# Eight tokens to a partition, one 128-token block and a new order in a linear-attention and ELU kernel

## The chip, the cores and the metric

The kernel runs on one core of a Trainium2 chip. The metric is the device time of one execution in microseconds (us), and lower is better. Three executions of the kernel before took 209.01, 209.1 and 213.92 us; their median is 209.1 us. A profile is one execution taken by the hardware profiler. Its engines are PE (TensorE matmuls; PEld is its weight loading), DVE (VectorE), ACT (ScalarE), POOL (GpSimd) and SP (SyncE, used here for DMA issue only).

## The reference, cut to what matters

There are 4 batches of 8 heads, 768 tokens and a head size of 64. Decayed linear attention goes in blocks of 64 tokens, and its output, heads side by side, goes through a two-layer network with an ELU.

```python
intra = (q_b @ k_b.T) * D          # D[i,j] = lam**(i-j) for i >= j, else 0; 64 x 64
out_b = intra @ v_b + (q_b * lam**(pos+1)) @ state
state = lam**64 * state + (k_b * lam**(63-pos)).T @ v_b
...
x = out as [4*768, 512]
h = x @ w_in                       # 512 -> 2048
g = where(h > 0, h, exp(min(h, 0)) - 1)
y = g @ w_out                      # 2048 -> 512
```

The first block of a batch has a state of zero, so the first 128 tokens need no state: one causal 128-token block with the decay `lam**(i-j)` gives the same values as two 64-token blocks.

## The kernel before, in words

The work is cut into 24 chunks of 128 tokens. Chunk g is token chunk g // 4 of batch g % 4, so chunks 0 to 3 are the first 128 tokens of the four batches. Chunks are handled in pairs (0, 2, 4 ... 22).

Nothing is scheduled by a planner at build time. `PROGRAM` is one string of words, and each engine executes its share of the words in that order. A set `ON` names the words that go to the other of two engines. A word is a kind, a pair or chunk number, sometimes a part, and after @ the PSUM banks that it opens:

- `L` loads a chunk of q or k (or a pair of v) through POOL's DMA queue with a cast to fp16; the pieces in memory are 256 bytes long, one token of one head. `wi` and `wo` load slices of the two weight matrices on the same queue. `H` loads a chunk uncast through SP and `C` casts it. `D` is a transpose by DMA, issued by SP.
- `T` and `t`: transposes of q and k on PE, and the copies of them out of PSUM. `S`: scores. `s` (and `z` for the first 64 queries of the first chunks): score times mask on DVE. `P` and `Q`: the products with v and with the state; `F` is a tiny DVE read that orders the two. `p`: the copy of the attention output to fp16, which is the network's input.
- `kd`: k times its decay. `U`: the products of decayed k and v. `M`: the state times lam^64, always on POOL. `u`: the new state, on DVE. For a pair of chunks these run as a chain `U`, `u.0`, `M.1`, `u.1`, then `M.0` of the next pair of the same batches.
- `A2:5` is the first matrix product of pair 2, piece 5 of 8 (8 matmuls). `x`: exp on ACT. `r`: relu on DVE or ACT. `m`: the ELU's join on DVE, which frees the PSUM bank and one of three buffers for exp results. `B7:3` is the second product of chunk 7, piece 3 of 4 (4 matmuls); `Ba` and `Bb` are halves of a piece. `o` and `st`: copy out and store.
- `W`: matmuls on zeros, which fill PE at the start.

Two things set the order around the change. Every engine, and POOL's DMA queue too, works strictly in the order of the words: an `M` that waits on POOL holds back the loads behind it. And at most eight of POOL's loads are under way; the ninth waits for the first.

In the first chunks `scores` makes three 64 x 64 products a head (late queries on late keys, late on early, early on early) into two kinds of banks (psS, psZ), `masked` and `masked_first` multiply them with masks that hold only the decay by key, and `evacuate_p` multiplies the decay by query (`qs`) in on the way out.

Of the kernel before, what the change touches and what calls it, by code (L numbers as in the profile page):

```python
# [99 lines left out]
def kernel(  # L100
# [545 lines left out]
```

## Time and profile before

| | us |
|---|---|
| median of the runs | 209.1 |
| the profiled execution | 208.75 |
| its span, first to last instruction | 206.6 |
| PE busy | 199.4 (97%) |
| DVE busy | 150.8 (73%) |
| POOL busy | 102.4 (50%) |
| ACT busy | 98.7 (48%) |
| first network matmul starts | 16.88 |

The profiled execution spends 2.15 us outside its span. Busy time is the time in which an engine executes something; for POOL it includes the issuing of DMAs here. PE is close to full, so a look at where PE waits, and for whom, says more than the other engines' shares.

### The profile page before, as it was taken

The numbers are of one execution on the slowest core, as the hardware profiler recorded it, in microseconds if no ns is written. First come the engines' busy times: TensorE is split into PE (matmuls) and PEld (weight loads), VectorE is DVE, ScalarE is ACT, GpSimd is POOL, SyncE is SP. The second block draws the span as 40 slices with busy tenths as digits, with TensorE's granted clock in tenths as the row PEclk, the third lists the DMA queues.
The fourth block names the chain that finished last, engine by engine and source line by source line (L and its number), as shares of the span: only waits on it lengthen the run. The fifth ranks groups of instructions, "written<-read, shape, count | busy, mean of one in ns | idle before, by whom it ended". The sixth has DMA issues, their size and how long they took to land.

```text
span 206.6 us, 6317 instructions
## 1 busy us (share of the span) xinstructions
PE 199.4 (97%) x2724; PEld 134.2 (65%) x2724; DVE 150.8 (73%) x251; ACT 98.7 (48%) x186; POOL 102.4 (50%) x107
## 2 busy tenths in 40 slices
PE   7888999999999999999999999999999999999993
PEld 2457887457656887676765686775666787767442
DVE  0498999959976789786677899768886377638730
ACT  3463589204730785645362286455332287557301
POOL 7997989889972999929940770360000000000000
PEclk9999999999999999999999999999999999999999
DMA  5999999999999999999999699674020041010007
GB/s 108 148 172 190 193 181 180 177 176 135 143 131 151 128 102 175 148 252 96 152 127 177 87 130 168 117 183 151 3 105 3 0 154 52 0 38 3 0 0 267
DMA packets 104443, 25.31 MB, mean 123 GB/s; under 512 B 95072, under 2 KB 101472, under 8 KB 104416
## 3 DMA queue, kind: packets, MB, share of 16 engines
q0 software_dynamic: 79008, 13.37, 101.4%
q1 hardware_dynamic: 25264, 11.54, 29.5%
q8 instruction: 21, 0.34, 0.7%
q14 instruction: 6, 0.05, 0.1%
q10 hardware_dynamic: 144, 0.00, 0.0%
HBM read 27.27 MB, written 6.29 MB: 162 GB/s over the span
## 4 chain that ended last, share of the span: by engine, by line
PE 91%; DVE 3%; DMA 3%; issue 1%; POOL 1%; ACT 0%; DVEq 0%; POOLq 0%
PE psH L487 41%; PE psM L520 40%; DMA kn<-in_k_dram 3%; PE psU L454 2%; PE psO L395 2%; PE psS L350 2%; PE psO L412 2%; DVE xt L430 1%; PE psO L383 1%; DVE ppz L362 1%; PE psTk L308 1%; POOL kn L290 1%; PE psMrest L558 0%; DVE loglam_p L185 0%; PE psTq L308 0%
## 5 line engine op out<-in xcount | busy, mean ns | idle before, releaser
L487 PE MATMUL psH<-xt,wi 128*128 128x256 f16 x768 | 91.5, 273 | 0.4 <-DVE xt L430 0.4
L495 ACT ACTIVATE e<-psH 128x512 f32<-128x512 f32 x96 | 55.5, 598 | 75.4 <-PE psH L487 44.8
L520 PE MATMUL psM<-wo,g 128*128 128x512 f16 (+1 forms) x384 | 90.3, 377 | 0.0
L487 PEld LDWEIGHTS <-wi 128*128 128x128 f16 x768 | 74.2, 98 | 16.0 <-issue 0.4
L506 DVE SCALAR_TENSOR_TENSOR g<-e,psH 128x512 f16<-128x512 f32 x96 | 63.3, 683 | 10.5 <-ACT psH L501 9.2
L520 PEld LDWEIGHTS <-g 128*128 128x128 f16 x384 | 36.5, 98 | 34.5 <-DVE g L506 0.2
L462 POOL TENSOR_TENSOR stt<-state,upp 128x512 f32<-128x512 f16 x20 | 21.9, 1101 | 31.5 <-DVE state L474 31.5
L499 DVE TENSOR_SCALAR psH<-psH 128x512 f32<-128x512 f32 x41 | 28.3, 694 | 8.2 <-ACT e L495 7.8
L501 ACT ACTIVATE psH<-psH 128x512 f32<-128x512 f32 x55 | 32.3, 596 | 0.0
L290 POOL DMA_DIRECT2D kn<-in_k_dram x24 | 22.0, 925 | 2.4 <-DMA wi<-in_moe_w_in_dram 1.5
L430 DVE TENSOR_TENSOR xt<-psO,qs 128x512 f16<-128x512 f32 x24 | 15.6, 684 | 8.8 <-PE psO L412 7.7
L290 POOL DMA_DIRECT2D qn<-in_q_dram x22 | 19.9, 916 | 0.0
L529 ACT COPY osb<-psM 128x512 f32<-128x512 f32 (+1 forms) x16 | 9.2, 580 | 21.3 <-PE psM L520 21.3
L358 DVE TENSOR_TENSOR pp<-psS,mask 128x512 f16<-128x512 f32 x24 | 16.2, 682 | 2.7 <-PE psS L350 2.6
L474 DVE TENSOR_TENSOR state<-stt,psU 128x512 f16<-128x512 f32 x20 | 13.4, 681 | 2.4 <-PE psU L454 1.6
L442 POOL TENSOR_TENSOR kd<-kn,ks 128x1024 f16<-128x1024 f16 (+1 forms) x7 | 14.3, 2050 | 0.9 <-DMA kn<-in_k_dram 0.9
L290 POOL DMA_DIRECT2D vn<-in_v_dram x12 | 14.3, 1188 | 0.0
L547 PE MATMUL psW<-zeros 128*128 128x512 f16 (+1 forms) x36 | 10.0, 431 | 1.2 <-DVE zeros L540 1.2
L529 DVE COPY osb<-psM 128x512 f32<-128x512 f32 x8 | 5.5, 690 | 6.2 <-PE psM L520 6.2
L547 PEld LDWEIGHTS <-zeros 128*128 128x128 f16 x36 | 3.7, 112 | 5.8 <-issue 2.8
L442 DVE TENSOR_TENSOR kd<-kn,ks 128x1024 f16<-128x1024 f16 (+1 forms) x5 | 6.5, 1309 | 0.0
L293 POOL DMA_DIRECT2D wi<-in_moe_w_in_dram x8 | 6.2, 824 | 0.0
(56 smaller groups left out, 80.5 us busy)
## 6 DMA issues: line engine op xcount, KB each, us to landing
out_dram<-osb SPq DMA_DIRECT2D x23, 256.0 KB, 2.6
kn<-in_k_dram POOLq DMA_DIRECT2D x24, 128.0 KB, 6.1
vn<-in_v_dram POOLq DMA_DIRECT2D x12, 256.0 KB, 8.6
qn<-in_q_dram POOLq DMA_DIRECT2D x22, 128.0 KB, 5.9
wi<-in_moe_w_in_dram POOLq DMA_DIRECT2D x8, 256.0 KB, 9.4
wo<-in_moe_w_out_dram POOLq DMA_DIRECT2D x8, 256.0 KB, 6.3
raw_q<-in_q_dram SPq DMA_DIRECT2D x2, 256.0 KB, 4.6
qT<-qn SPq DMA_TRANSPOSE x18, 5.0
```

Source lines behind the costliest of these rows:

```text
L290: nc.gpsimd.dma_start(out=dst, in_=source(w, g0, n))
L358: nc.vector.tensor_tensor(out=p[:], in0=psS.pop(g)[:], in1=m[:], op=ALU.mult)
L430: nc.vector.tensor_tensor(out=xg[g0][:, :, a + s : a + 4 : 2, :].rearrange("p k i t -> p i k t"), in0=psO.pop((g, s))[:], in1=qs[:].unsque ...
L442: (nc.vector if f"kd{g}" in ON else nc.gpsimd).tensor_tensor(out=kds[g][r], in0=of("k", g)[r], in1=ks[r].unsqueeze(2).unsqueeze(3).broadca ...
L462: nc.gpsimd.tensor_tensor(out=t[:], in0=state[b, 2 * cb + s][:], in1=upp[:].unsqueeze(2).broadcast_to([128, H, 64]), op=ALU.mult,)
L487: nc.tensor.matmul(pH[:, f * n * 128 : (f + 1) * n * 128], lhsT=wi16[i][:, kk, w * 128 : (w + 1) * 128], rhs=xg[g0][:, kk].rearrange("p a ...
L495: nc.scalar.activation(es[g0, j][:], psH[g0, j][:], AF.Exp)
L499: nc.vector.tensor_scalar_max(psH[g0, j][:], psH[g0, j][:], 0.0)
L501: nc.scalar.activation(psH[g0, j][:], psH[g0, j][:], AF.Relu)
L506: nc.vector.scalar_tensor_tensor(out=g[:].rearrange("p f c t -> p (f c t)"), in0=es.pop((g0, j))[:], scalar=-1.0, in1=psH.pop((g0, j))[:], ...
L520: nc.tensor.matmul(psM[g][:, cols], lhsT=gts[g, f], rhs=wo16[i][:, w, cols], start=f == 0, stop=f == NFT - 1, skip_group_check=True,)
L529: (nc.vector.tensor_copy if on_dve else nc.scalar.copy)(o[:], src)
```

## The change

For chunks 0 to 3, q and k are loaded a second way: partition 16 h + o holds tokens 8 o to 8 o + 7 of head h, so that each piece in memory is 2 KB long. Chunks 0 and 1 (`H`) come uncast through SP, chunks 2 and 3 (`G`) as fp16 through POOL; both are then copied into tiles `oct` by `C`. The transposes work on pairs of such tiles, one for each of the eight token places, and the copies out of PSUM put the tokens back in order with a stride. The ordinary loads of k (`Lk0` to `Lk3`) stay, for `kd`, at later places; the old loads of q for chunks 0 to 3 (two raw ones on SP, `Lq2` and `Lq3`) go away.

The scores of the first chunks are one 128 x 128 product a head, in two halves of four heads (`Sz`, `S`), and the products with v are also in two halves (`Pz`, `P`). The mask of these chunks, 128 x 128 for each head, now holds the causal cut and the whole decay: eight exps on ACT (`dcz`, `dcs`) and two products on DVE (`mkz`, `mks`). So `p` is a plain copy there, on ACT for pair 0 and on DVE for pair 2. `llp` moves to ACT.

`PROGRAM` and `ON` are new throughout. 34 instead of 41 relus are on DVE, 7 instead of 5 `kd` (kd0, kd2 and kd4 among them, which POOL did before) and 9 instead of 8 `o`.

```diff
+EIGHTS = [('k', 0), ('k', 2), ('q', 0), ('q', 2)]
...
+    def decays(heads):
+        for h in heads:
+            nc.scalar.activation(mask1[:, h, :], dist[:], AF.Exp, scale=loglam[:, h : h + 1])
+    def mask_first(heads):
+        m = mask1[:, heads.start : heads.stop, :]
+        nc.vector.tensor_tensor(
+            out=m, in0=m, in1=cau1[:].unsqueeze(1).broadcast_to([128, len(heads), L]), op=ALU.mult
+        )
...
+    def eights(w, g):
+        c, b = divmod(g, B)
+        x = {"q": q, "k": k}[w][b, :, c * L : (c + 1) * L]
+        p = g - g % 2
+        if (w, p) not in oct:
+            oct[w, p] = buf(f"oct{w}{p}", [128, 8, 2, 64], FP16, f"oct{w}{p}")
+        return x.rearrange("h (o j) d -> h o (j d)", j=8), oct[w, p][:, :, g % 2]
...
+    def load_eights(w, g):
+        raw[w, g] = buf(f"stg{w}{g}", [128, 8, 64], FP16, f"stg_{w}{g}")
+        nc.gpsimd.dma_start(out=flat(raw[w, g][:]), in_=eights(w, g)[0])
...
+        if (w, g) in EIGHTS:
+            src = src.rearrange("p j x -> p x j")
+            dst = tr[w, g][:].rearrange("p h (o j) -> p (h o) j", j=8)[:, :, r.start : r.stop]
...
+    def scores_first(g, heads, store, banks):
+        for i in range(2):
+            store[g + i] = bank(banks[i], [128, H // 2, L], FP32, f"psS{g + i}_{heads.start}")
+        for n, h in enumerate(heads):
+            for i, d in enumerate(R):
+                nc.tensor.matmul(
+                    store[g + i][:, n, :], lhsT=tr["k", g][d, h, :], rhs=tr["q", g][d, h, :],
+                    start=True, stop=True, skip_group_check=True,
+                )
...
+    def first_chunk_products(g, x, banks):
+        psO[g, x] = bank(banks[0], [128, NHP // 2, 2, L], FP32, f"psO{g}_{x}")
+        for i in range(2):
+            for n in range(NHP // 2):
+                for c, rc in enumerate(R):
+                    nc.tensor.matmul(
+                        psO[g, x][rc, n, i, :], lhsT=vof(g + i)[:, x * NHP + 2 * n + c, :],
+                        rhs=(pp if x else ppz)[g + i][:, 2 * n + c, :], start=True, stop=True,
+                        skip_group_check=True,
+                    )
...
+        if g < B:
+            (nc.vector.tensor_copy if f"p{g}.{s}" in ON else nc.scalar.copy)(
+                xg[g0][:, 2 * s : 2 * s + 2, a : a + 4, :].rearrange("p k a t -> p k (a t)"),
+                psO.pop((g, s))[:].rearrange("p k i t -> p k (i t)"),
+            )
+            return
```

The two orders, as far as the prediction speaks of them (a line of dots marks what is left out):

```diff
-    "wz W0@0 W1 W2 W3 W4 W5 W6 W7 W8 W9 W10 W11 W12 W13 W14 W15 Lk0 lam Lk1 tab Lv0 Lk2 iota Hq0 "
-    "Lk3 ln row Lq2 Lq3 pos1 wi7 wi2 Lv2 wi1 wi6 Hq1 wi3 Cq0 pos0 pos5 dn1 pos2 pos3 cau1 idn "
-    "pos4 wi0 wi4 W16 W17 W18 Cq1 Tqa0@1 Tka0@2 tqa0 tka0 Tkb0 Tqb0 W19 W20 W21 W22 tqb0 llp tkb0 "
-    "S0@3,4,5,6 W23 W24 W25 qs dn W26 W27 W28 W29 ks kd0 msk1 W30 Tk2@7 tk2 W31 up W32 Tq2@1 tq2 "
-    "cau s1 msk z0 s0 z1 P0@2,4 p0.0 p0.1 S2@5,3,7,6 z3 A0:7@1 A0:2@2 s2 z2 s3 P2@4,6 p2.0 p2.1 "
-    "U0@5,7 W33 W34 W35 A0:1@3 x0:2 x0:7 r0:2 u0.0 r0:7 m0:7 m0:2 A2:7@0 x0:1 r0:1 wo0 Lq4 A2:2@4 "
-    "wi5 x2:2 x2:7 r2:7 r2:2 A0:6@6 A2:1@5 A2:6@1 m0:1 x0:6 r0:6 m2:7 m2:2 m0:6 x2:1 A0:0@2 "
-    "A2:0@3 x2:0 r2:1 m2:1 A2:4@0 r2:0 m2:0 x2:6 A2:3@4 A0:4@6 r2:6 x0:0 m2:6 r0:0 x2:4 Lk4 kd2 "
-    "Lk5 M0.1 wo6 x2:3 Ba2:0@5 Lq5 Ba3:0@3 m0:0 r2:3 u0.1 m2:3 A0:3@1 A0:5@2 Tk4@7 x0:4 r2:4 m2:4 "
...
+    "Hq1 wz W0@0 W1 W2 W3 W4 W5 W6 W7 W8 W9 W10 Hk0 wi2 Gq2 Gk3 iota pos0 row idn Gk2 Gq3 pos1 "
+    "pos2 dis Lv0 lam tab wi0 Lv2 wi1 wi5 Lq4 wi6 Lq5 wi3 Lk4 cau1 wi4 wi7 Lk5 ln dcz up Ck0 Lk0 "
+    "wo0 Lk1 wo1 wo2 wo3 Hq0 pos3 Cq0 Hk1 Ck1 W11 W12 W13 W14 W15 W16 W17 W18 Tka0@1 W19 Cq1 "
+    "Tqa0@2 Tkb0@3 dcs W20 tqa0 tka0 Cq2 Ck3 tkb0 cau pos4 mkz mks W21 Tqb0@4 tqb0 Ck2 Cq3 W22 "
+    "W23 W24 W25 W26 W27 Sz0@5,6 W28 Tka2@7 tka2 Tqa2@1 S0@2,3 W29 Tkb2@4 z0 W30 Tqb2@5 tqa2 tkb2 "
+    "z1 W31 W32 Pz0@7 s0 s1 P0@6 tqb2 Sz2@1,2 z2 S2@4,3 W33 W34 p0.0 p0.1 W35 A0:0@5 z3 Pz2@7 s3 "
+    "A0:2@6 s2 P2@0 p2.0 dn x0:2 p2.1 r0:2 A0:1@1 x0:1 m0:2 A2:2@2 r0:1 x0:0 r0:0 A2:0@3 x2:2 "
+    "r2:2 m2:2 m0:0 m0:1 A2:5@4 A0:6@7 x0:6 r0:6 Tq4@0 x2:0 r2:0 A0:5@6 x0:5 A2:6@2 A2:1@5 m2:0 "
+    "r0:5 ks x2:6 r2:6 m0:5 m0:6 m2:6 x2:1 r2:1 A0:3@1 msk A2:3@3 x0:3 A0:7@6 m2:1 x2:5 r2:5 r0:3 "
+    "Tk4@7 A2:4@2 x2:3 r2:3 m0:3 m2:5 m2:3 tq4 A2:7@5 tk4 A0:4@1 kd0 x2:4 r2:4 x0:4 r0:4 Ba0:0@4 "
+    "S4@0,3 s4 s5 m2:4 Ba1:0@7 Bb0:0 Bb1:0 U0@0,3 Ba0:1 Ba1:1 u0.0 Lv4 wo5 Ba2:0@2 wo7 Ba3:0@0 "
+    "Bb3:1 Bb0:1 kd4 wo6 M0.1 Lk6 u0.1 M4.0 Lk7 x0:7 llp qs x2:7 Bb2:0 r2:7 Ba3:1 r0:7 Bb1:1 m0:7 "
+    "m0:4 U4@3,6 Ba2:1 u4.0 Bb2:1 m2:7 Q4.1@1,3 F4 Bb2:2 P4 wo4 Bb0:3 Bb2:3 p4.0 p4.1 Bb0:2 Bb3:3 "
+    "Bb3:0 A4:0@5 Lk2 Bb3:2 A4:7@1 M4.1 Ba2:3 u4.1 x4:7 x4:0 r4:0 Ba3:2 A4:5@3 Ba3:3 Ba0:3 x4:5 "
+    "Ba0:2 Ba2:2 m4:0 Dk6.0 o3 r4:7 A4:1@6 Lq6 Lq7 x4:1 r4:5 m4:7 Lk3 kd2 M8.0 A4:3@5 r4:1 x4:3 "
+    "o0 r4:3 Ba1:2 A4:4@0 m4:5 A4:6@1 Lk8 o2 Dq6.0 U2@4,3 m4:3 m4:1 x4:6 Lv6 u2.0 r4:6 x4:4 r4:4 "
+    "kd6 U6@2,5 A4:2@6 x4:2 Dq6.1 B4:0@4 m4:6 r4:2 m4:4 Bb1:2 Lk9 B4:3 B4:2 Dk6.1 Lq8 Lq9 Dk8.0 "
+    "Lv8 Lk22 M2.1 u2.1 M6.0 kd8 B5:0@1 B5:3 m4:2 u6.0 Q6.1@0,3 F6 S6@6,2 Ba1:3 B5:1 s6 s7 P6 "
...
```

More of the change, by code (lines that the diff above doesn't have):

```diff
@@ L18 @@
 EARLY = 0
+EIGHTS = [('k', 0), ('k', 2), ('q', 0), ('q', 2)]
 BUFS = {'qn': 5, 'kn': 5, 'vn': 6, 'qT': 4, 'kT': 4, 'pp': 6, 'kd': 3, 'state': 6, 'stt': 3, 'xt2': 3, 'xt4': 2, 'e': 3, 'g': 40, 'osb512': 6}
 WARM = [512, 512, 512, 512, 512, 512, 512, 512, 512, 512, 512, 512, 512, 512, 512, 512, 512, 512, 512, 512, 512, 512, 512, 512, 512, 512, 512, 512, 512, 512, 256, 256, 256, 256, 256, 256]
-ON = {'Cq0', 'r14:6', 'r10:5', 'o17', 'r22:3', 'r0:0', 'r8:6', 'r20:6', 'r20:1', 'r0:1', 'r18:2', 'Cq1', 'o12', 'r12:4', 'o18', 'r6:6', 'r10:1', 'r4:7', 'r14:4', 'o19', 'r22:6', 'r14:5', 'kd20', 'lam', 'r2:1', 'kd18', 'r18:0', 'r2:5', 'r18:6', 'r16:7', 'r4:1', 'kd12', 'tqb0', 'r20:3', 'r18:7', 'r4:2', 'o4', 'r12:2', 'r22:0', 'o20', 'kd6', 'r2:0', 'r4:0', 'tqa0', 'o11', 'kd8', 'r14:1', 'r10:3', 'r8:2', 'r12:0', 'r6:2', 'r6:7', 'r18:5', 'r4:6', 'r0:3', 'r0:7', 'r0:4', 'r4:5', 'o13'}
+ON = {'r22:3', 'kd16', 'Cq3', 'r18:3', 'o18', 'r20:5', 'r22:4', 'kd0', 'o17', 'kd20', 'r16:5', 'r0:5', 'r8:6', 'r0:3', 'r8:4', 'r18:0', 'r10:7', 'r12:7', 'Ck2', 'r4:5', 'o19', 'r8:2', 'o13', 'r16:0', 'lam', 'r8:5', 'kd2', 'r20:3', 'p2.0', 'r0:1', 'Cq1', 'r16:2', 'r18:4', 'r10:5', 'o1', 'r22:6', 'r6:4', 'kd8', 'r12:1', 'r4:6', 'r0:0', 'o14', 'r2:2', 'r22:0', 'r18:2', 'tka0', 'kd14', 'r18:7', 'r10:1', 'r0:2', 'r14:6', 'o16', 'kd4', 'o3', 'r0:6', 'o0', 'p2.1'}
 PROGRAM = (
[56 rows of a table removed]
[57 rows of a table added]
 )
@@ L150 @@
     mask = const("mask", [128, H, LB])
-    cau1 = const("cau1", [128, LB])
-    dn1 = const("dn1", [128, H])
-    mask1 = const("mask1", [128, H, LB])
+    cau1 = const("cau1", [128, L])
+    dist = const("dist", [128, L])
+    mask1 = const("mask1", [128, H, L])
     qs = const("qs", [128, NHP, LB])
@@ L167 @@
     HEADS = {"": range(H), "a": range(H // 2), "b": range(H // 2, H)}
-    nat, raw, tr, psT, psS, pp, psO, xg = {}, {}, {}, {}, {}, {}, {}, {}
+    nat, raw, oct, tr, psT, psS, pp, psO, xg = {}, {}, {}, {}, {}, {}, {}, {}, {}
     kds, stt, psU, psH, es, gts, psM, osb = {}, {}, {}, {}, {}, {}, {}, {}
@@ L230 @@
         ),
-        "pos5": lambda _: nc.vector.tensor_scalar(
-            out=pos[:, 5:6], in0=pos[:, 0:1], scalar1=-1.0, scalar2=float(LB), op0=ALU.mult, op1=ALU.add
+        "dis": lambda _: nc.vector.tensor_scalar(
+            out=dist[:], in0=row[:], scalar1=pos[:, 0:1], scalar2=0.0, op0=ALU.subtract, op1=ALU.max
         ),
-        "dn1": lambda _: nc.scalar.activation(dn1[:], loglam[:], AF.Exp, scale=pos[:, 5:6]),
         "cau1": lambda _: nc.vector.tensor_scalar(
-            out=cau1[:], in0=row[:, :LB], scalar1=pos[:, 5:6], scalar2=0.0, op0=ALU.add, op1=ALU.is_ge
+            out=cau1[:], in0=row[:], scalar1=pos[:, 0:1], scalar2=None, op0=ALU.is_ge
         ),
-        "msk1": lambda _: nc.vector.tensor_tensor(
-            out=mask1[:],
-            in0=cau1[:].unsqueeze(1).broadcast_to([128, H, LB]),
-            in1=dn1[:].unsqueeze(2).broadcast_to([128, H, LB]),
-            op=ALU.mult,
-        ),
+        "dcz": lambda _: decays(HEADS["a"]),
+        "dcs": lambda _: decays(HEADS["b"]),
+        "mkz": lambda _: mask_first(HEADS["a"]),
+        "mks": lambda _: mask_first(HEADS["b"]),
         "ks": lambda _: nc.scalar.activation(ks[:], loglam[:], AF.Exp, scale=pos[:, 4:5]),
@@ L271, in vof, with flat @@
         return nat["v", g - g % 2][:, :, g % 2]
+    def eights(w, g):
[5 more added lines that the diff above has]
+        return x.rearrange("h (o j) d -> h o (j d)", j=8), oct[w, p][:, :, g % 2]
+    def flat(t):
+        return t.rearrange("p j d -> p (j d)")
     def load_raw(w, g):
-        raw[w, g] = buf(f"raw{w}{g}", [128, H, 64], FP32, f"raw_{w}{g}")
-        (nc.scalar if f"H{w}{g}" in ON else nc.sync).dma_start(
-            out=raw[w, g][:], in_=source(w, g, 1)
-        )
+        raw[w, g] = buf(f"raw{w}{g}", [128, 8, 64], FP32, f"raw_{w}{g}")
+        (nc.scalar if f"H{w}{g}" in ON else nc.sync).dma_start(out=flat(raw[w, g][:]), in_=eights(w, g)[0])
     def cast_raw(w, g):
-        t = nat_tile(w, g)[:, :, g % 2]
+        t = eights(w, g)[1]
         if f"C{w}{g}" in ON:
@@ L305, in transpose @@
         if banks[0]:
-            psT[w, g] = bank(banks[0], [128, H, 128], FP16, f"psT{w}{g}")
+            psT[w, part, g] = bank(banks[0], [128, H, 128], FP16, f"psT{w}{part}{g}")
         for h in HEADS[part]:
             nc.tensor.transpose(
-                psT[w, g][:, h, :], in_=of(w, g)[:, h, :, :], identity=ident16[:]
+                psT[w, part, g][:, h, :],
+                in_=oct[w, g][:, h, :, :] if (w, g) in EIGHTS else of(w, g)[:, h, :, :],
+                identity=ident16[:],
             )
@@ L316, in evacuate_t @@
         dst = tr[w, g][:, r.start : r.stop, :]
-        src = psT[w, g][:, r.start : r.stop, :]
+        src = psT[w, part, g][:, r.start : r.stop, :]
+        if (w, g) in EIGHTS:
+            src = src.rearrange("p j x -> p x j")
+            dst = tr[w, g][:].rearrange("p h (o j) -> p (h o) j", j=8)[:, :, r.start : r.stop]
         if f"t{w}{part}{g}" in ON:
@@ L330, in transpose_dma @@
         )
+    def scores_first(g, heads, store, banks):
[7 more added lines that the diff above has]
+                )
     def scores(g, banks):
+        if g < B:
+            scores_first(g, HEADS["b"], psS, banks)
+            return
         for i in range(2):
             psS[g + i] = bank(banks[i], [128, H, LB], FP32, f"psS{g + i}")
-        if g < B:
-            for i in range(2):
-                psZ[g + i] = bank(banks[2 + i], [128, H, LB], FP32, f"psZ{g + i}")
-            for h in range(H):
-                for kb, qb in ((1, 1), (0, 1), (0, 0)):
-                    for i, d in enumerate(R):
-                        nc.tensor.matmul(
-                            (psS if qb else psZ)[g + i][R[kb], h, :],
-                            lhsT=tr["k", g][d, h, R[kb]], rhs=tr["q", g][d, h, R[qb]],
-                            start=True, stop=True, skip_group_check=True,
-                        )
-            return
         for h in range(H):
@@ L355, in masked, with masked_part, out_bank @@
     def masked(g):
+        if g < B:
+            masked_part(g, HEADS["b"], psS, pp)
+            return
         p = pp[g] = buf("pp", [128, H, LB], FP16, f"pp{g}")
-        m = mask1 if g < B else mask
-        nc.vector.tensor_tensor(out=p[:], in0=psS.pop(g)[:], in1=m[:], op=ALU.mult)
-    def masked_first(g):
-        p = ppz[g] = buf("pp", [128, H, LB], FP16, f"ppz{g}")
-        nc.vector.tensor_tensor(out=p[R[0]], in0=psZ.pop(g)[R[0]], in1=mask[R[0]], op=ALU.mult)
-    def out_banks(g, banks):
-        for s in range(2):
-            psO[g, s] = bank(banks[s], [128, 2, NHP, LB], FP32, f"psO{g}_{s}")
+        nc.vector.tensor_tensor(out=p[:], in0=psS.pop(g)[:], in1=mask[:], op=ALU.mult)
+    def masked_part(g, heads, src, dst):
+        p = dst[g] = buf("pp", [128, H // 2, L], FP16, f"pp{g}_{heads.start}")
+        nc.vector.tensor_tensor(
+            out=p[:], in0=src.pop(g)[:], in1=mask1[:, heads.start : heads.stop, :], op=ALU.mult
+        )
+    def masked_first(g):
+        masked_part(g, HEADS["a"], psZ, ppz)
+    def out_bank(g, s, b):
+        psO[g, s] = bank(b, [128, 2, NHP, LB], FP32, f"psO{g}_{s}")
+    def first_chunk_products(g, x, banks):
[8 more added lines that the diff above has]
+                    )
     def products(g, banks):
@@ L377, in products @@
         if cb == 0:
-            out_banks(g, banks)
-            for s, rows, p in ((0, R[0], ppz), (1, slice(None), pp)):
-                for i in range(2):
-                    for hp in range(NHP):
-                        for c, rc in enumerate(R):
-                            nc.tensor.matmul(
-                                psO[g, s][rc, i, hp, :], lhsT=vof(g + i)[rows, 2 * hp + c, :],
-                                rhs=p[g + i][rows, 2 * hp + c, :], start=True, stop=True,
-                                skip_group_check=True,
-                            )
+            first_chunk_products(g, 1, banks)
             return
@@ L405, in state_products @@
         if part == 1:
-            out_banks(g, banks)
+            for s in range(2):
+                out_bank(g, s, banks[s])
             early[f"Q{g}.1"] = set(done)
@@ L429, in evacuate_p @@
         a = 2 * (g - g0)
+        if g < B:
+            (nc.vector.tensor_copy if f"p{g}.{s}" in ON else nc.scalar.copy)(
+                xg[g0][:, 2 * s : 2 * s + 2, a : a + 4, :].rearrange("p k a t -> p k (a t)"),
+                psO.pop((g, s))[:].rearrange("p k i t -> p k (i t)"),
+            )
+            return
         nc.vector.tensor_tensor(
@@ L573 @@
             simple[name](None)
-        elif kind in ("Hq", "Hk", "Hv"):
+        elif kind in ("Hq", "Hk"):
             load_raw(kind[1], *a)
-        elif kind in ("Cq", "Ck", "Cv"):
+        elif kind in ("Cq", "Ck"):
             cast_raw(kind[1], *a)
+        elif kind in ("Gq", "Gk"):
+            load_eights(kind[1], *a)
         elif kind in ("Lq", "Lk", "Lv"):
@@ L585 @@
             transpose_dma(kind[1], *a)
+        elif kind == "Sz":
+            scores_first(*a, HEADS["a"], psZ, banks)
         elif kind == "S":
             scores(*a, banks)
+        elif kind == "Pz":
+            first_chunk_products(*a, 0, banks)
         elif kind == "P":
```

2 lines of the change are left out of this document (1 added, 1 removed), and 86 rows, old and new, of the table PROGRAM.

## The prediction, made before the result was known

> **What bounds the kernel now.** I read the chain that ended last first, then the waits of PE, then the timeline of the first 60 us. By line the chain of the page's part 4 begins:
>
> ```profile
> PE 91%; DVE 3%; DMA 3%; issue 1%; POOL 1%; ACT 0%; DVEq 0%; POOLq 0%
> ```
>
> Nine tenths of the span are PE's own work. The longest pieces of that chain show where the rest is:
>
> ```profile
> 2.32 5.65 DMA kn<-in_k_dram
> ...
> 16.88 1.91 PE psH L487 x16
> 18.78 0.35 PE psO L383 x12
> 19.13 0.46 issue
> 19.59 0.62 PE psO L383 x20
> 20.21 0.38 PE psU L454 x32
> 20.59 0.43 PE psW L547 x3
> 21.02 9.61 PE psH L487 x88
> ```
>
> (start, length, what). Up to 16.88 the chain goes from the load of k through transposes, masks and DVE; at 16.88 the network starts, and from 21.02 PE is not idle again: the waits of PE, asked for from 40 to 65 us, are an empty list, and busy time by stretch gives PE 20.00 of 20 us from 42 to 62, 37.99 of 38 up to 100, 50.00 of 50 up to 150. So only two things can move the time: how much PE has done by about 21 us, and new waits of PE behind it. Matmuls cost the same in both kernels: 88 matmuls of A in 9.61 us are 0.873 us for a piece of 8, and the last 56 of B, 12.09 us, are 0.432 for a half.
>
> **The head.** The chunks' loads no longer decide it. SP issues its raw loads 0.51 us apart from 0.74, so the fourth starts at 2.3. Loads in 2 KB pieces are not in the trace; the stores of 256 KB are, with 2 KB pieces, and land in 2.6 us; the raw loads in 256-byte pieces landed in 4.1 and 5.0. That bounds the fourth load between 4.9 and 7.3; I take 6. Its cast on DVE (not shown for fp32 from SBUF; 0.42 for a 128x512 fp16 copy, 0.69 for any fp32 one) ends before 8. But PE can't begin its transposes before W18, and 19 W took from 1.19 to 7.53 us. From there I add up PE's own list up to A0:0: eight half transposes of 0.39 (3.1), eleven W of 512 at 0.22 (2.4), six of 256 at about 0.13 (0.8), four score blocks and two product blocks. The blocks are new in shape: 16 matmuls of 128 columns, against 8 transposes of 128 columns in 0.61 us, would be 1.2 one after another and 0.3 if they overlapped as fully as the 64 x 64 ones; two at a time, the nearest, 0.44, and 0.35 for a product block. Sum 8.8: **A0:0 at 16.3**, bounds 15.8 to 19. Beside it DVE (five casts, `tka0`, `mkz`, `mks` and four masks at a pitch of 0.61) is through with `s1` at 14.4 and ACT with `p0.1` at 15.9, so neither is late unless a load is. The mask's eight exps on ACT (0.34 each by the qs rows, 128x64) lie beside PE's W, and `p` of pair 0, an ACT copy of 0.6, takes the place of a DVE product of 0.69. Four loads are more than before (k of chunks 0 to 3 comes twice), and the small-piece loads of k move behind 20 us, where POOL's issue and PE's work hide them up to `kd0` and `kd2`, which are priced below.
>
> Behind A0:0 the kernel before lost time: its products of pair 2 waited for masks, and its third A started at 21.02. Now Pz2, A0:2, P2 and A0:1 follow with their masks done in time (`s2` ends at 18.1), and A2:2 follows `p2.1` at 19.65. By then three A and the products are done; before, that plus U0 (0.38) was done at 21.02 + 0.87. **Gain so far 1.9 us.**
>
> **The stage up to Q4.1.** Here the changed order does 16 A in a row and only then B, with U0 behind them; before, U0 came at 20.14, behind two A. DVE's list from `r0:2` (19.5) is 20 operations up to `m2:3`. The page's relu and ELU rows are 0.69 long, but follow each other at 0.61 (`g` x3 in 1.88): 12.1 us, to 31.6. Buffers of exp results and ACT leave no longer gap by my reading, list against list. PE, which needs those banks, reaches S4 at 32.6. Then `kd0`, on DVE now, 1.22 as at 60.77 (the cover that it had before, POOL, is gone); `s4` and `s5` to 34.5, and U0, which takes their banks, at 34.6; `m2:4`, `u0.0` to 35.8. Now the state's chain: M0.1 on POOL meets `kd4` on DVE. The trace has one such meeting:
>
> ```profile
> 45.93 3.02 POOL L462 TENSOR_TENSOR stt<-state,upp 128x512 f32<-128x512 f16 x2 [0.89 <-DVE state L474]
> 46.37 1.69 DVE L442 TENSOR_TENSOR kd<-kn,ks 128x1024 f16<-128x1024 f16 x1
> 54.81 0.45 PE L454 MATMUL psU<-vn,kd 64*64 64x64 f16 x32
> ```
>
> Two M in 3.02 us, the longest 2.01 against 1.03 else. So M0.1 ends at 37.85, `u0.1` at 38.55, M4.0 (behind Lk6) at 39.85, `u4.0` at 40.6: **Q4.1 at 40.7**. PE's own list from 16.3 gives 39.7 (16 A 14.0, 15 halves 6.5, products 0.7, two U 0.76, two transposes 1.0, S4 0.47), so PE waits 1.0 us here. Before, Q4.1 started at 41.69 with one half less done. The Trainium skill, page "SBUF — State Buffer", section "Who interferes with whom", says that a VectorE instruction with two SBUF inputs and a GpSimd one that reads SBUF exclude each other for the whole instruction; by that, M0.1 would only begin when `kd4` ends and everything behind it would be 0.6 us later still; the row above shows the slowing, and not whether one waits for the other's end.
>
> **The stage up to U6** decides. POOL's queue is in order: Lk6, Lk7, wo4, Lk2, Lq6, Lq7, Lk3, Lk8 and Lv6 stand behind M0.1, M4.0, M4.1 and M8.0. Before, `M0.1` was done at 25.1 and the vn of pair 6 was issued at 43.88, eleven us ahead of its U6 at 54.81 (third row above). Now POOL has nothing to do from about 30 (28 loads at 0.73 to 1.19 from 1.27) to 35.8. From M4.0's end at 39.85: Lk7 0.93, wo4 0.74, Lk2 0.93, M4.1 1.05, three loads 2.8, M8.0 1.05, Lk8 0.93: **Lv6 is issued at 48.25.** How long it takes is this row and its neighbours:
>
> ```profile
> vn<-in_v_dram POOLq DMA_DIRECT2D x1, 256.0 KB, 8.6
> ...
> DMA to landing us min/median/max: 6.6/8.4/13.3
> ```
>
> (the first from the DMA issues of 34 to 48 us, the second from the tile vn over the first 60 us; a single one from 60 to 80 us took 6.0.) By 8.4 it lands at 56.65. PE reaches U6 13.2 us after Q4.1 (7 A 6.1, 14 halves 6.05, U2, Q4.1, P4 together 1.1), at 53.9, and waits 2.7. `kd2` in front of it (k of chunk 3 issued at 45.4, landing 5.5, then 1.22) lets U2 go at about 53.5, as PE comes. So U6 is at 56.65, with one half (0.43) more done than before at 54.81: **1.4 us late**. A wait of 1 us at Q4.1 and 2.7 at U6 eats the 1.9.
>
> **The rest.** Behind U6 both lists hold the same A, B and attention work, and the loads of pairs 8 and 10 come 1 to 3 us before they are used by the same adding; I add nothing. Relus move 7 x 0.65 us from DVE to ACT, `kd` and `o` move some 4 us back; both engines have room (73% and 48%). The end is the same: 11 pieces of B after the last A against 14 before, each more than the evacuation of A needs.
>
> Sum: 208.75 + 1.4 = 210.2 for the profiled execution; the median of the runs before is 0.35 above it, so **210.5**.
>
> **Rivals.**
> - *The gain is kept.* POOL's loads have little beside them at 48 us, and Lv6 lands in 6.0: U6 at 54.25, 1.0 us ahead of before: 208.1. If the wait at Q4.1 went too, 207.1. For it: POOL's pause before 36 lets the DMA rings run empty. Against: 18 transposes by DMA and the small pieces of q and k fill the same engines (busy share of 9 tenths up to half the span).
> - *Slower: loads behind the state chain.* The same mechanism with 13.3, the longest landing of a v in this trace: U6 at 61.55, 6.3 us late: 215.4. It passes 2% (213.3) from a landing of 11.2. Lk9, Lq8, Lq9 and Lv8 stand in the same queue behind `kd6`, so it can strike again at U8. For it: POOL's order. Against: a median of 8.4.
> - *The new loads are not early.* Eight loads and wi2 start together; wi, in 1 KB pieces, took 6.1 to 11.1 to land. With 9 us the fourth raw load lands at 11.3, its transpose starts 3.6 to 4 us late, and all else with it: 1.4 + 3.6 gives 214. Against: only a few loads are under way at 2 us.
>
> **How the numbers follow.** Forecast (209.2 to 213.3) 0.48; gain kept (206.7 to 209.2) 0.27; loads behind the chain (213.3 to 216.5) 0.14; late raw loads (211 to 215) 0.08, half of it above 213.3; something faster than 204.9 that I don't see, 0.03: PE's list alone allows 16.3 + 23.4 = 39.7 at Q4.1, 2.4 us better than before with its extra half, not the 4.2 that 2% needs. 2% is about what a measurement of this kernel tells from no change. Range 207.4 to 214.3, which leaves out some 0.07 below and 0.10 above. Faster 0.03, same 0.79, slower 0.18.
>
> **What would show it.** In the profile after: first A at 16.3, and no gap of PE before the fourth A; a wait of PE for DVE around U0 to Q4.1; the vn of pair 6 issued near 48 and a wait of PE on it of 1 to 4 us near 55; PE full from there on. A first A at 18 or later, gaps of PE above 2 us before 41, or any idle PE behind 65 us would make the forecast wrong.

## The result and the profile after

The changed kernel is slower: a median of 216.78 us in four runs (216.02 to 217.43) against 210.45 in four runs of the kernel before. The ratio is 1.032, with a 95% interval of 1.022 to 1.043; it leaves out one disturbed run of the kernel before (213.92), which is why it is a little above the ratio of the two medians. The profiled execution took 216.02 us, its span 214.0, which is 7.4 us more than the span before.

The chain that ended last, by engine, from the page of the kernel after:

```profile
PE 61%; DMA 12%; DVE 10%; POOL 10%; issue 3%; ACT 1%; SPq 1%; DVEq 0%; POOLq 0%; ACTq 0%
```

It was nine tenths PE before. Now DMA, DVE and POOL carry a third of it. For the beginning I asked for the chain up to 62 us (start, length, what):

```profile
2.91 11.13 DMA raw_k<-in_k_dram
14.06 0.44 DVE octk L305
14.54 0.61 PE psTka L333 x4
...
23.68 0.87 PE psH L533 x8
```

The fourth raw load is issued at 2.91 and holds everything for 11.13 us. The network's first matmul, at 16.88 before, is at 23.51 (the chain shows its last stretch, from 23.68). PE's waits, over the first 24 us, name one new wait (line, releaser, us, times, longest):

```profile
PE psTka L333 <- DVE octk L305: 7.3, 1, 7.3
```

The longest waits of the head before were 1.2 us for the zeros, which is still there, and 0.8. The four casts of the raw loads, from the timeline of DVE and of ACT (start, length, engine, line, operation, then in brackets the idle time before it and what ended it):

```profile
6.42 0.60 ACT L303 CAST octq<-raw_q 128x512 f16<-128x512 f32 x1
...
8.60 0.43 DVE L305 CAST octk<-raw_k 128x512 f16<-128x512 f32 x1 [3.50 <-DMA raw_k<-in_k_dram]
...
11.71 0.43 DVE L305 CAST octq<-raw_q 128x512 f16<-128x512 f32 x1 [2.62 <-DMA raw_q<-in_q_dram]
...
14.06 0.43 DVE L305 CAST octk<-raw_k 128x512 f16<-128x512 f32 x1 [1.92 <-DMA raw_k<-in_k_dram]
```

The three on DVE each wait for their load, so their starts are the landings: 3.1 and 2.35 us apart, though SP issued the loads 0.6 to 0.9 us apart. (The first load, cast on ACT, was there by 6.42.) They do not land side by side but one after another.

Busy time by stretch shows a second effect. The columns are the stretch, then for PE, PEld, DVE, ACT and POOL the busy us and (instructions), then the granted clock, the DMA share and GB/s:

```profile
10.00:12.00 2.00, 0.00 (x0) 0.00 (x0) 0.29 (x1) 0.00 (x0) 0.76 (x1) 0.93 1.59 220
12.00:14.00 2.00, 0.00 (x0) 0.00 (x0) 0.14 (x1) 0.00 (x0) 0.74 (x1) 0.50 1.68 179
14.00:16.00 2.00, 1.46 (x11) 1.18 (x12) 1.24 (x3) 0.00 (x0) 1.43 (x2) 0.50 1.89 176
16.00:18.00 2.00, 2.00 (x13) 1.16 (x11) 1.94 (x6) 1.33 (x3) 1.84 (x3) 0.50 1.62 156
18.00:20.00 2.00, 2.00 (x16) 0.79 (x15) 0.15 (x1) 1.37 (x3) 0.89 (x1) 0.86 1.72 169
```

PE went idle at 7.3. About 4.5 us later the granted clock fell to a half, and it stayed there for 4 us after PE began its transposes. The Trainium skill, page "TensorE: Matmul & The Clock Gate", section "Part 1: The HAM clock gate (the "warmup" mystery)", says that the clock halves after an idle window of some 3.4 us and returns after as much sustained work; the rows above, 4.5 and 4 us, lie about a microsecond above that.

Where the time went, by stages (us; Q4.1 and U6 are those of the forecast, and the second column adds up the prediction's own steps):

| | predicted | measured |
|---|---|---|
| first A starts | 16.3 | 23.51 |
| first A to Q4.1 | 24.4 | 24.42 (to 47.93) |
| Q4.1 to U6 | 15.95 | 13.82 (to 61.75) |
| U6 to the end of the execution | 153.5 | 154.27 |
| sum | 210.15 | 216.02 |

So the head is 7.2 us later than forecast, and the stage up to U6 gives 2.1 of that back. The rest is 0.8.

### The profile page after: what moved, and what is told of

It is laid out like the page before. It is cut to its first block, busy times and chain, and to the rows that moved or that the text cites. A ratio compares the mean times of both kernels' runs of the same rounds, so it can differ in the third digit from the quotient of the medians.

```text
span 214.0 us, 6149 instructions
## 1 busy us (share of the span) xinstructions
PE 201.2 (94%) x2628; PEld 134.7 (63%) x2628; DVE 149.4 (70%) x248; ACT 105.6 (49%) x207; POOL 99.3 (46%) x107
## 4 chain that ended last, share of the span: by engine, by line
PE 61%; DMA 12%; DVE 10%; POOL 10%; issue 3%; ACT 1%; SPq 1%; DVEq 0%; POOLq 0%; ACTq 0%
PE psM L566 28%; PE psH L533 23%; DMA vn<-in_v_dram 5%; DMA raw_k<-in_k_dram 5%; DVE g L552 5%; POOL kn L315 2%; POOL stt L508 2%; DVE psH L545 2%; PE psW L593 2%; POOL qn L315 2%; POOL kd L488 2%; DMA kn<-in_k_dram 2%; PE psO L452 1%; PE psU L500 1%; POOL vn L315 1%
## 5 line engine op out<-in xcount | busy, mean ns | idle before, releaser
L508 POOL TENSOR_TENSOR stt<-state,upp 128x512 f32<-128x512 f16 x20 | 22.9, 1149 | 35.9 <-DVE state L520 27.1
L547 ACT ACTIVATE psH<-psH 128x512 f32<-128x512 f32 x62 | 36.5, 597 | 0.0
L545 DVE TENSOR_SCALAR psH<-psH 128x512 f32<-128x512 f32 x34 | 23.2, 694 | 9.1 <-ACT e L541 8.8
L315 POOL DMA_DIRECT2D qn<-in_q_dram x20 | 18.0, 908 | 0.6 <-DMA stg_k<-in_k_dram 0.6
L476 DVE TENSOR_TENSOR xt<-psO,qs 128x512 f16<-128x512 f32 x20 | 13.0, 685 | 5.8 <-PE psO L452 5.8
L391 DVE TENSOR_TENSOR pp<-psS,mask 128x512 f16<-128x512 f32 x20 | 13.1, 683 | 1.1 <-PE psS L381 1.0
L593 PE MATMUL psW<-zeros 128*128 128x512 f16 (+1 forms) x36 | 11.7, 460 | 1.2 <-DVE zeros L586 1.2
L488 POOL TENSOR_TENSOR kd<-kn,ks 128x1024 f16<-128x1024 f16 (+1 forms) x5 | 9.7, 1934 | 2.5 <-DMA kn<-in_k_dram 2.5
L488 DVE TENSOR_TENSOR kd<-kn,ks 128x1024 f16<-128x1024 f16 (+1 forms) x7 | 9.9, 1419 | 0.0
L333 PE MATMUL psTka<-ident,octk 128*128 128x128 f16 x8 | 1.0, 262 | 7.3 <-DVE octk L305 7.3
```

The source lines that it names most:

```text
L315: nc.gpsimd.dma_start(out=dst, in_=source(w, g0, n))
L391: nc.vector.tensor_tensor(out=p[:], in0=psS.pop(g)[:], in1=mask[:], op=ALU.mult)
L488: (nc.vector if f"kd{g}" in ON else nc.gpsimd).tensor_tensor(out=kds[g][r], in0=of("k", g)[r], in1=ks[r].unsqueeze(2).unsqueeze(3).broadca ...
L508: nc.gpsimd.tensor_tensor(out=t[:], in0=state[b, 2 * cb + s][:], in1=upp[:].unsqueeze(2).broadcast_to([128, H, 64]), op=ALU.mult,)
L545: nc.vector.tensor_scalar_max(psH[g0, j][:], psH[g0, j][:], 0.0)
L547: nc.scalar.activation(psH[g0, j][:], psH[g0, j][:], AF.Relu)
```

## The experiments

My theory: SP's queue passes the four raw loads one behind another, and beside POOL's first loads it gets only a part of the DMA engines, so that the fourth is late. Rivals: the shape of the pieces, the amount of POOL's bytes ahead of them, SP's queue alone, and the clock. Unless a median is given, a run below is one execution; executions of the kernel before lay between 208.66 and 214.22 us, so the readings rest on times inside the traces more than on the totals.

**POOL's loads held back.** A copy on POOL that waits for the fourth raw load stands ahead of all its loads; the raw loads are the first four on SP in any case.

```diff
-Hk0 wi2 Gq2 Gk3 iota pos0 ... Hq0 pos3 Cq0 Hk1 Ck1
+Hk0 Hq0 Hk1 iota hold wi2 Gq2 Gk3 pos0 ... pos3 Cq0 Ck1
+    def hold(_):
+        nc.gpsimd.tensor_copy(t[:], raw["k", 1][:, 0, :1])
```

> All loads of POOL's queue are held back until the fourth raw load has landed. Theory (the raw loads share the DMA engines with the loads that POOL starts at the same time, 1.6 MB by 8 us): with nothing beside them the four land one behind the other by 5 to 7 us, so the first transpose starts at about 7.5 instead of 14.5; the loads of chunks 2 and 3 and of the weights then come later, and the first network matmul may still not be early. Rival 1 (loads in 2 KB pieces on SP's queue are slow by themselves, some 2.7 us each): the fourth lands at 11 to 14 as before. Rival 2 (SP's queue passes only one load at a time): four steps of over 2 us, 10 us or later.

Measured: 219.29 us, first transpose at 11.22, first A at 26.59. The raw loads' casts, from the timelines of ACT and DVE:

```profile
5.63 0.62 ACT L303 CAST octq<-raw_q 128x512 f16<-128x512 f32 x1 [0.62 <-DMA raw_q<-in_q_dram]
...
7.36 0.43 DVE L305 CAST octk<-raw_k 128x512 f16<-128x512 f32 x1 [4.98 <-DMA raw_k<-in_k_dram]
...
9.07 0.43 DVE L305 CAST octq<-raw_q 128x512 f16<-128x512 f32 x1 [1.22 <-DMA raw_q<-in_q_dram]
10.74 0.43 DVE L305 CAST octk<-raw_k 128x512 f16<-128x512 f32 x1 [1.24 <-DMA raw_k<-in_k_dram]
```

All four start when their load lands, 1.7 us apart: 256 KB in 1.7 us is some 155 GB/s, with nothing else of size under way. So both explanations hold a part. Even alone the fourth lands at 10.7, not at the 5 to 7 that I expected; the sharing adds 3.3 us to that. The bytes by queue say the same. From the DMA view of 4 to 8 us (queue, packets, MB, share of 16 engines), first of this run, then of the kernel after, where q1 is SP's queue and q0 POOL's:

```profile
q1 hardware_dynamic: 333, 0.65, 53.1%
```

```profile
q0 software_dynamic: 683, 0.32, 74.2%
q1 hardware_dynamic: 232, 0.44, 37.4%
```

SP's queue moved 0.65 MB in 4 us alone, and 0.44 MB with POOL's queue beside it. Alone it kept the 16 DMA engines only 53% busy, so there it is not full engines that space the loads; what in the queue does is not shown. The time is worse than that of the kernel after because everything on POOL was held back: behind the first transposes PE waits another 4.79 us for the copies of the next chunks.

**Piece size.** The same loads in pieces of one token of one head (256 bytes), with the copies out of PSUM in plain order.

```diff
-return x.rearrange("h (o j) d -> h o (j d)", j=8), oct[w, p][:, :, g % 2]
+return source(w, g, 1), oct[w, p][:, :, g % 2]
```

> The same loads on the same queues in the same order, but in 256-byte pieces, one token of one head a partition and head (the transposes then give heads instead of token places, and the copies out of PSUM need no new order). Theory (the bytes under way decide): no earlier, first transpose at 14 to 18 us. Rival (large pieces on SP's queue are what is slow): first transpose near 8, as in the kernel before, and the first network matmul near 16 to 18.

Measured: 216.0 us, first transpose at 14.18, first A at 23.04. The piece size neither makes the loads late nor would cure them.

**Clock.** 32 more matmuls on zeros ahead of the first transpose.

```diff
+WARM += [512] * 32
-W18 Tka0@1
+W18 W36 W37 ... W67 Tka0@1
```

> 32 more matmuls on zeros between the last of the old ones and the first transpose (7 us), so that PE does not idle while it waits for the raw loads. Theory (the late load is the loss, and PE's half clock after the idle 7.3 us comes on top): the granted clock stays at 1.0 and the time from the first transpose to the first network matmul shrinks from 9.0 to 7 to 8 us, so 1 to 2 us of the 7.4 are the clock's. Rival (DVE and ACT set that stretch): 9.0 as it was, time unchanged at 216.

Measured: 215.55 us. The granted clock was 1.00 throughout. The last raw load landed 1.1 us later in this run (first transpose at 15.64), but first transpose to first A took 7.04 us instead of 8.97. The half clock costs 1.9 us of the head here; it follows from the idle PE and is not the cause.

**k on ACT's queue.** The two raw loads of k are issued by ACT, those of q by SP.

```diff
-Hk0 wi2 ... Hq0 pos3 Cq0 Hk1 Ck1
+Hk0 Hq0 Hk1 wi2 ... pos3 Cq0 Ck1
+ON has Hk0 and Hk1 (ACT issues them)
```

> The two raw loads of k go through ACT's DMA queue, and all four are issued at the start. Theory (shared engines): both queues get a share beside POOL's, so the fourth lands some 2 to 3 us earlier, near 11, and the time falls by as much, to 213 to 214. Rival 2 (one load at a time on SP's queue): two and two in parallel, the fourth lands near 7 to 8 us and the time falls to about 210.

Measured: 215.87 us, first A at 23.51 as in the kernel after; neither explanation had expected that. k of chunk 0 was cast at 5.27 and the first transpose came at 12.71 instead of 14.54, but the second load of q landed only at 11.89, and what was won was lost again. Part of that is a side effect of the edit: the small load of the decays is on ACT's queue too, now behind k. ACT read it at 3.48 in the kernel after, and here:

```profile
12.46 0.21 ACT L185 ACTIVATE loglam<-lam_b 128x8 f32<-128x8 f32 x1 [7.87 <-DMA lam_b<-in_lam_dram]
```

ACT then cast q of chunk 1 at 13.98 instead of 6.42, PE waited another 0.9 us for it, and the granted clock was 0.50 from 14 to 18 us. So this run does not tell what a third queue alone is worth.

**Only POOL's order.** The raw loads stay on SP; POOL's first loads are put in the order in which they are needed, the weights last.

```diff
-wi2 Gq2 Gk3 iota pos0 row idn Gk2 Gq3 ... Lv0 ... wi0 Lv2 wi1
+Gk2 Gq2 iota pos0 row idn Lv0 Gk3 Gq3 wi0 wi2 Lv2 ... wi1
```

> The four raw loads stay on SP; of POOL's first loads only the order is new: Gk2, Gq2, the tables, Lv0, Gk3, Gq3, wi0, wi2, Lv2, instead of wi2, Gq2, Gk3, the tables, Gk2, Gq3, Lv0, wi0, Lv2. Theory (the raw loads share the DMA engines with whatever else is under way, so fewer bytes beside them bring them in earlier): wi2 reads 512 KB and a G 256 KB; about 1 to 1.5 us less beside the raw loads, first transpose at 13 to 13.5 instead of 14.54, first A at 22 or so, time 214.5 to 215.5. Rival (SP's queue by itself passes them this slowly when any other queue has work): first transpose at 14.5, time 216.

Measured: 217.2 us, first transpose at 15.29, first A at 24.66. My theory failed here in its form "fewer bytes beside them": with other loads first on POOL's queue, the raw loads came no earlier, and even a little later than the rival had it. SP's casts on DVE were 2.9 and 2.7 us apart, as if the two queues took turns. The Trainium skill, page "DMA: Bandwidth & Descriptors", section "Queues, rings and completion order", says that each DMA engine goes round-robin between the queues that have work, a packet at a time. The bytes by queue fit that: from 4 to 8 us SP's queue moved 0.44 MB here, as in the kernel after, and 0.65 MB alone. The turns themselves are not in the trace.

**Two of the four on POOL.** As the run above, with k of chunks 0 and 1 loaded by POOL (first in its queue, in the same 2 KB pieces), so that SP carries only q.

```diff
-Hq1 wz ... Hk0 Gk2 Gq2 iota ... Hq0 pos3 Cq0 Hk1 Ck1
+Hq1 Hq0 wz ... Gk0 Gk1 Gk2 Gq2 iota ... pos3 Cq0 Ck1
```

> k of chunks 0 and 1 goes through POOL (as Gk0, Gk1, first in its queue, 2 KB pieces), so that SP carries only q; everything else is as in the order run. Theory (what was late is the fourth raw load, behind 768 KB on one queue and beside POOL's first loads): k0 and k1 land at 7 to 8, q0 at about 7.5, first transpose at 8 to 9, first A at 17 to 18, time 210 to 211: all 6 us or nearly all come back. Rival (the same 1 MB must be read for the pair, and the engines give it 150 to 200 GB/s whatever the queue): first transpose 11 or later, time 213 or above.

Measured: 210.12 us. From the timelines of DVE and PE:

```profile
7.92 0.29 DVE L305 COPY octk<-stg_k 128x512 f16<-128x512 f16 x1 [1.87 <-DMA stg_k<-in_k_dram]
...
9.04 0.43 DVE L305 CAST octq<-raw_q 128x512 f16<-128x512 f32 x1 [0.77 <-DMA raw_q<-in_q_dram]
9.38 0.29 DVE L305 COPY octk<-stg_k 128x512 f16<-128x512 f16 x1
...
9.72 0.40 PE L333 MATMUL psTka<-ident,octk 128*128 128x128 f16 x4 [2.33 <-DVE octk L305]
...
12.83 0.38 DVE L305 COPY octk<-stg_k 128x512 f16<-128x512 f16 x1 [1.78 <-DMA stg_k<-in_k_dram]
...
18.20 1.04 PE L533 MATMUL psH<-xt,wi 128*128 128x256 f16 x8
```

The second load of q is now the last of its queue and lands at 9.0; first transpose at 9.72, first A at 18.20, and the clock stayed at 1.00, since 2.33 us of idle did not lower it. Timed beside the kernel before (six runs, median 210.28, against 209.57 in fifteen):

> The run with k0 and k1 on POOL again, timed beside the kernel before: 0.99 to 1.01 of it by its first look (210.12 against 210.63).

The ratio is 1.0047, interval 1.0029 to 1.0065: of the 3.2% only 0.5% is left, with the new block, mask, copies and order all in place.

**With twelve matmuls more.** The same with 2.6 us of matmuls on zeros ahead of the first transpose.

```diff
+WARM += [512] * 12
-W18 Tka0@1
+W18 W36 W37 ... W47 Tka0@1
```

> The run before this one with twelve more matmuls of 512 columns on zeros (2.6 us) ahead of the first transpose. Theory (half a clock behind an idle PE costs up to 1.9 us between first transpose and first A): if the loads land at 8 to 9, PE is idle for 1 us at most without the new matmuls, the clock stays up in both, and this one is 0 to 1.5 us later than it; if the first transpose is at 11 or later without them, this one is about 1 to 1.5 us faster.

Measured: 210.15 us, first A at 18.02. There was no half clock to cure, and the fill cost nothing.

**Three on SP.** Only k of chunk 1 on POOL.

```diff
-Hq1 Hq0 wz ... Gk0 Gk1 Gk2 Gq2
+Hq1 Hk0 Hq0 wz ... Gk1 Gk2 Gq2
```

> As the run with k0 and k1 on POOL, but only k1 goes there; SP carries three raw loads (q1, k0, q0). Theory (beside POOL's loads SP's queue passes one of these 256 KB loads per 2.6 to 2.9 us, so the time depends on how many stand in it): the third lands about 2.7 us behind the second, q0's cast at 11.5 to 12.2, first transpose at 12 to 12.8, first A at 20.5 to 21.5, between the 18.2 of two raw loads and the 23.5 to 24.7 of four; time 212.5 to 213.5. Rival (k0 and k1 on POOL helped because POOL's first loads no longer were ahead of something, not by SP's count): first transpose at 9.7 again or at 14.5 again.

Measured: 214.82 us, first A at 22.00. The timelines of DVE and PE:

```profile
9.27 0.43 DVE L305 CAST octk<-raw_k 128x512 f16<-128x512 f32 x1 [3.80 <-DMA raw_k<-in_k_dram]
...
12.61 0.43 DVE L305 CAST octq<-raw_q 128x512 f16<-128x512 f32 x1 [2.85 <-DMA raw_q<-in_q_dram]
...
13.30 0.55 PE L333 MATMUL psTka<-ident,octk 128*128 128x128 f16 x4 [5.19 <-DVE octk L305]
```

The third load lands 3.3 us behind the second. Between two and four loads on SP lies a time between the two, so beside POOL's queue it is the number of loads in SP's that decides. (With ACT's queue at work as well, in the run with k on ACT, the second load of q landed at 11.89 instead of 9.04, so the place in the queue is not all.) It came 0.4 to 1.3 us above what I expected at every point: the landing was later, and PE, idle for 5.19 us, met the lower clock (0.68 on average from 12 to 16 us), which I had left out.

**The same from the other side.** The kernel before with one change, two slices of the weights first on POOL's queue.

```diff
-wz W0@0 ... W15 Lk0 lam Lk1 ... wi7 wi2
+wz W0@0 ... W15 wi7 wi2 Lk0 lam Lk1 ...
```

> The kernel before with one change: wi7 and wi2 (512 KB read each) are the first two loads on POOL's queue, ahead of Lk0. Theory (loads that stand ahead share the engines and the queue): k0 and k1 are issued 2 us later and land 2 to 4 us later; the first network matmul moves from 16.88 to 19 to 21, and the time is 2 to 4 us above the kernel before on the same chip. Rival (the chunk loads of the kernel before are slow for their 256-byte pieces and not for what stands beside them): k lands 2 us later by its issue and no more, the first A at about 18.5.

Measured: 215.13 us against 210.63, first A at 22.13 instead of 16.88. PE's waits in the first 24 us:

```profile
PE psTk L308 <- DMA kn<-in_k_dram: 2.1, 1, 2.1
PE psO L383 <- DVE ppz L362: 1.5, 2, 0.9
PE psTq L308 <- ACT qn L282: 1.3, 1, 1.3
```

k is issued 1.67 us later, and its first transpose comes 3.1 us later (11.18 against 8.11). That is more than the issue, as the theory has it. The total of 5.25 us is more than I expected: the clock was 0.50 from 12 to 14 us, though PE's longest wait was 2.1 (it was busy for only 0.8 of the 4 us from 8 to 12), and the tables and masks, behind the same loads, came later too. How the total divides between these was not separated. What it shows is that the head of the kernel before, too, hangs on what stands ahead of its loads.

**An order made from this.** The tables and v of pair 0 between k1 and k of chunk 2 on POOL, and on DVE the two mask products ahead of the copies of chunks 2 and 3. In the rows of the run with two on POOL, DVE waited 1.78 us for chunk 3 at 12.83, and the masks stood behind it.

```diff
-Gk0 Gk1 Gk2 Gq2 iota pos0 row idn Lv0 Gk3
+Gk0 Gk1 iota pos0 row idn Lv0 Gk2 Gq2 Gk3
-Ck0 Lk0 ... tqa0 tka0 Cq2 Ck3 tkb0 cau pos4 mkz mks W21
+Ck0 mkz Lk0 ... tqa0 tka0 mks Cq2 Ck3 tkb0 cau pos4 W21
```

> The same with two changes of order. On POOL the tables and v of pair 0 come between k1 and k of chunk 2, so that fewer loads stand beside the first ones; on DVE the two mask products come ahead of the copies of chunks 2 and 3 (in the run with k0 and k1 on POOL, DVE waited 1.78 us for chunk 3's load at 12.83, did the masks' 1.28 us only behind it, and z0 came at 14.55 although its scores were done at 13.06). Theory: z0 at 13.1 or a little earlier, first A at 16.5 to 17, and as nothing behind waits for long the end comes as much earlier: 208.5 to 209, about 1.2 us below the run with k0 and k1 on POOL. Rival (what is gained at the head is lost at the chain of DVE up to 30 us or at the loads of pair 6): 210.

Measured: a median of 209.79 us in ten runs, ratio 1.003 with an interval of 0.9996 to 1.0065. First A came at 17.56 and the first mask product at 13.77: 0.6 us came of the 1.2 that I expected, since k of chunk 3 landed later (13.33). This is level with the kernel before and does not beat it.

All the profiled kernels in one table: the time of the profiled execution less the start of the first A.

| | first A | time | difference |
|---|---|---|---|
| POOL held | 26.59 | 219.29 | 192.70 |
| POOL's order only | 24.66 | 217.20 | 192.54 |
| kernel after | 23.51 | 216.02 | 192.51 |
| k on ACT | 23.51 | 215.87 | 192.36 |
| small pieces | 23.04 | 216.00 | 192.96 |
| more matmuls on zeros | 22.68 | 215.55 | 192.87 |
| kernel before, weights first | 22.13 | 215.13 | 193.00 |
| three on SP | 22.00 | 214.82 | 192.82 |
| two on POOL | 18.20 | 210.12 | 191.92 |
| two on POOL, timed again | 18.18 | 210.47 | 192.29 |
| two on POOL, more on zeros | 18.02 | 210.15 | 192.13 |
| new order | 17.56 | 209.55 | 191.99 |
| kernel before | 16.88 | 208.75 | 191.87 |

Over 9 us of difference at the head, the rest varies by 1.1 us. What the head loses is lost at the end, and nothing behind it takes it up. The row of the kernel before adds something: behind its first A it needs no longer than any of the changed ones, so by these runs the new order won nothing there.

## Why the prediction was wrong

**The step that failed** is "The chunks' loads no longer decide it ... That bounds the fourth load between 4.9 and 7.3; I take 6." The fourth raw load was cast at 14.06. I priced each load by the time that a load or a store takes from issue to landing and let the four overlap in full, as if only the issues followed each other. The two raw loads of the kernel before did hold a sign of it: issued 0.51 us apart, they landed 4.1 and 5.0 us later, so 1.4 us apart. At that pace a fourth load would land at about 9.1, an estimate from these rows, and not at 6. The run with POOL held shows 1.7 us for each load in SP's queue even without company, which put the fourth at 10.7, and the kernel after 2.35 to 3.1 us with POOL's queue beside it.

**A term that was missing** is the clock. I had the transposes at the full clock; PE's idle 7.26 us halved it, for 1.9 us, by the run with more matmuls on zeros.

**The rival "The new loads are not early"** named the right place and had a chance of 0.08. Its price, 9 us to land, was read from loads of weights in this profile; the fourth load took 11.1 us, and it left out the clock. So even this rival came to 214 (215 at most), and the range ended at 214.3, under the fastest of the four runs, 216.02. My reason against it, "only a few loads are under way at 2 us", was wrong twice: four of 256 KB in one queue suffice, and by 5 us POOL's queue held five more.

**The list from there to A0:0** was too long, and came out near by accident. I had 8.8 us, and the kernel after took 8.97, but with half the clock in it. In the run with 32 more matmuls on zeros, where the clock was full and all the chunks had landed, it took 7.04; the 8.48 of the run with two on POOL have DVE's wait for chunk 3 in them. The term is the half transposes: I took 0.39 for each, which is the length of one record, but records overlap. From the timeline of PE in the run with 32 more matmuls:

```profile
15.64 0.40 PE L336 MATMUL psTka<-ident,octk 128*128 128x128 f16 x4 [1.27 <-DVE octk L308]
15.88 0.38 PE L596 MATMUL psW<-zeros 128*128 128x512 f16 x1
16.09 0.39 PE L336 MATMUL psTqa<-ident,octq 128*128 128x128 f16 x4
16.32 0.39 PE L336 MATMUL psTkb<-ident,octk 128*128 128x128 f16 x4
...
18.59 0.40 PE L370 MATMUL psS<-qT,kT 64*128 64x128 f16 x8
18.91 0.39 PE L596 MATMUL psW<-zeros 128*128 128x512 f16 x1
```

From start to start a half transpose takes 0.23 us, so eight are 1.3 us less; a block of scores takes 0.32 and not 0.44, which is 0.5 for four.

**The stage up to Q4.1** was right to 0.02 us: 24.42 against 24.4. The path was right too: counted from the first A, M0.1 ended at 21.7 (forecast 21.55), `u4.0` at 24.4 (24.3), and Q4.1 began 0.05 us behind it. Only PE's own work was longer than I had it, 24.1 us busy where my list had 23.4, so of the 1.0 us that I had it wait ahead of Q4.1 no wait of PE shows. The stage includes the meeting on SBUF, which I had at 2.0 us for M0.1. From the timelines of DVE and POOL of the kernel after:

```profile
43.07 1.21 DVE L488 TENSOR_TENSOR kd<-kn,ks 128x1024 f16<-128x1024 f16 x1
43.31 1.88 POOL L508 TENSOR_TENSOR stt<-state,upp 128x512 f32<-128x512 f16 x1 [8.73 <-DVE state L518]
...
45.22 0.69 DVE L520 TENSOR_TENSOR state<-stt,psU 128x512 f16<-128x512 f32 x1 [0.93 <-POOL stt L508]
```

M0.1 starts 0.24 us behind `kd4` and ends 0.91 us after it; the next three, undisturbed, take 1.05 to 1.08. So it did little or nothing while `kd4` ran, which fits the exclusion that the Trainium skill's page "SBUF — State Buffer" (section "Who interferes with whom") states, weighed in the prediction as 0.6 us more. By the end of M0.1 rule and row come to the same here, because the row that I took had the wait in it. POOL's pause ahead of M0.1 was there too, 8.73 us of it where I had some 6.

**The stage up to U6** was mis-sized. Lv6 was issued at 55.23, 7.3 us behind Q4.1, as the list had it (7.55), but v of pairs 6 and 8 landed in 6.4 to 6.6 us and not in 8.4, and PE waited 0.25 us instead of 2.7. From the timelines of POOL and PE:

```profile
55.23 1.16 POOL L315 DMA_DIRECT2D vn<-in_v_dram  x1
...
61.75 0.44 PE L500 MATMUL psU<-vn,kd 64*64 64x64 f16 x32 [0.25 <-DMA vn<-in_v_dram]
```

Without the late loads this might have been my rival "The gain is kept": 16.3 and the 192 to 193 of the table give 208.3 to 209.3, against 208.75 before. The first A at 17.56 is the earliest that any changed kernel reached, so whether these loads can be had in time for 16.3 stays open.

**The rest** cost 0.8 us that I had at nothing. PE's waits behind U6 show 0.26 us for DVE ahead of a block of scores at 105.4 and 0.16 behind it; what the other 0.35 are stays open.

## What to carry to other kernels

The 256 KB loads on SP's queue landed one behind another here. So price the last of several loads by its place in the queue, the bytes ahead of it on that queue, and the rate that the queue gets beside the others, and not by the latency of a single load. Ahead of a kernel's first matmul, put what is needed first on the queues so that none of them holds more than its part; a new order on another queue did nothing here for a load that waited in its own. A PE that idles for 5 us or more, or does very little for as long, was paid for twice in these runs, once as idle time and once as matmuls at half the clock.

## What the runs showed of the hardware

- SP's queue alone passed four loads of 256 KB at 1.7 us each, some 155 GB/s; with POOL's queue busy, at 2.35 to 3.3 us. Pieces of 2 KB and of 256 bytes made no difference that could be seen (first transpose at 14.54 and 14.18).
- Spreading loads over queues won no bytes a second in total but gave the waiting load its turn: k on POOL's queue brought the first transpose from 15.29 to 9.72. The Trainium skill, page "DMA: Bandwidth & Descriptors", section "Rules for kernel authors", says that spreading over the issuing engines does not help for bandwidth. From 4 to 8 us both runs moved 195 and 196 GB/s, which agrees; the time still fell by 7 us.
- The granted clock was still 1.00 after 2.33 and after 3.27 us of idle PE, and at 0.50 after 7.26 us. In the runs with POOL held and with three on SP, PE was back at work after 4.79 and 5.19 us and the clock still fell to 0.50 some 0.1 to 0.3 us later, an estimate from the means over 2 us.
- It need not be one long wait: in the kernel before with the weights first, PE's longest wait was 2.1 us, but PE was busy for 0.8 of the 4 us from 8 to 12, and the clock was 0.50 from 12 to 14.
